# First chunk of a windowed-attention and gated-convolution kernel taken from plain fp32 to three reduced passes, with a ring of 27 blocks for the late queries and keys

## The chip, the cores and the metric

The kernel runs on one core of a Trainium2 chip. The metric is the device time of one execution, in microseconds (us); lower is better. Times of before are given as the median of three executions.

## What is computed

The reference has two halves. The first is causal attention with a window of 128 tokens and a linear distance bias, for 8 batches, 8 heads, 576 tokens and 64 columns per head:

```python
scores = scale * np.matmul(q, k.transpose(0, 1, 3, 2))
rel = pos[:, None] - pos[None, :]
mask = (rel >= 0) & (rel < window)
scores = np.where(mask, scores + bias[None], -1000000000.0)
attn = softmax(scores); attn_out = np.matmul(attn, v)
```

The heads are then laid side by side to x of 4608 tokens by 512, and the second half is a gated network with a depthwise convolution of three taps along the tokens of a batch:

```python
h = np.maximum(x @ w_in, 0.0)                  # 512 -> 1024
conv_out = sum(conv_w[k] * hp[:, k:k + S, :] for k in range(3))
out = h * sigmoid(conv_out) @ w_out            # 1024 -> 512
```

The inputs q and k are scaled so that the scores are large; the weights of the network come as float64 and are decoded on the chip.

## The kernel before

**Tiles and chunks.** Attention goes by 36 tiles `t` of 128 tokens. The network goes by 18 chunks `c` of 256 tokens (two tiles), and within a chunk by four steps, `s = 4c .. 4c+3`, each of two blocks of 128 of the 1024 inner columns. `up(s, ff)` is x times w_in (PSUM tile `p`), `relu`, `middle`, `conv_side` (twice), `tanh` and `gate` make the gated value `z`, `g_hi` and `g_lo` split z into a high and a low half (`gh`, `gl`), and `down(s)` multiplies by w_out into the PSUM tiles `o`.

**Two ways to multiply.** Steps of chunks 1 to 17 multiply in three reduced-precision passes over halves: high weight by high data, high weight by low data, low weight by high data (line 697 in `up`, line 804 in `down`). The halves of x lie in a ring of two chunks, `ring`, filled by `x_hi` and `x_lo`; the halves of the weights are `wi`, `wo` (high, `w_hi`) and `wl` (low, `w_lo`). Chunk 0 (`s < NFP`, with NFP = 4) multiplies in plain fp32, by the whole decoded weight `wg` and by whole data, one matmul in the program per block:

```python
if s < NFP:
    nc.tensor.matmul(
        ps, wgs[b].bitcast(F32)[:, part], x_first[:, cc], start=cc == 0, stop=cc == NCC - 1
    )
    continue
```

A plain fp32 matmul stands as two rows in the profile.

**The weights.** Sixteen blocks of weights and one of taps come by DMA into staging tiles (`wst`, 6 buffers) and are decoded by `w_clamp` (POOL), `w_rebias` (ACT), `w_low` (ACT or DVE), `w_bits` (DVE), `w_hi` (ACT or POOL) and `w_lo` (POOL or DVE).

**Queries and keys.** Tiles 0 to 7 are loaded by `load` and turned by TensorE (`qkT`). From tile 8 on they are loaded in blocks of 32 tokens by 32-row pieces and turned on DVE by `turn` (line 365). A group is 9 blocks (`GB = 9`) in a tile `rp_late` with two buffers: 32 DMAs of 36 KB a group, line 315, emitted by `load_some` where the order has an `LG4`. All DMAs are issued by SP, in order, as are the scratch write of the attention weights (`scr`), the four skewed reads of it (`rr`), the values (`rv`) and the output (`ob`).

**The order.** Nothing is scheduled automatically. Three strings of pieces, `OPENING` (up to about tile 10 and step 9), `PERIOD` (two tiles and one chunk, 14 times) and `TAIL`, are emitted under `tc.manual_schedule`; each engine runs its instructions in that order. A piece is a letter code and numbers: `UH0.1` is `up(0, 1)`, `D5` is `down(5)`, `GH`/`GL` are `g_hi`/`g_lo`, `XH`/`XL` are `x_hi`/`x_lo`, `W` is `w_lo`, `TQ` is `turn`, `WE`/`SE` write and read the scratch, `AV` is attention times values, `S` the scores, `OB` the output. The set `OTHER` names the pieces that `pick` sends to the second of two possible engines.

Of the kernel before, what the change touches and what calls it, by code (L numbers as in the profile page):

```python
# [22 lines left out]
def tile_alibi_window_attention_conv_glu(  # L23
# [71 lines left out]
    mh = apool.tile([P, P], F32, name="mh", tag="qk", bufs=2)  # L95
# [8 lines left out]
    ma = apool.tile([P, P], F32, name="ma", tag="qk", bufs=2)  # L104
# [5 lines left out]
    dist = apool.tile([P, P], F32, name="dist", tag="qk", bufs=2)  # L110
# [16 lines left out]
    for name, cuts in (("start", (96, 64, 32, 0)), ("half", (None, None, 96, 64)), ("after", (32, 0, None, None))):  # L127
        m = apool.tile([P, P], F32, name=f"w_{name}_f", tag="qk", bufs=2)
# [45 lines left out]
    NST = 6  # L174
# [3 lines left out]
    NWL = 18  # L178
# [95 lines left out]
    x_first = apool.tile([P, NCC, XW], F32, name="x_first", tag="xx", bufs=1)  # L274
    nc.vector.memset(x_first[:, :, 0:1], 0.0)
# [13 lines left out]
    TURN = FIRST  # L289

    GB = 9
    groups, turned = {}, [TURN]

    def loads():
        for n in range(TURN * NB // GB, NT * NB // GB):
            lo, hi = max(n * GB, TURN * NB), (n + 1) * GB
            b, s = divmod(lo * BK, S)
            for i, src in enumerate((k, q)):
                for a in range(2):
                    for half in range(D // BK):  # L300
# [22 lines left out]
    def early_raw(t):  # L323
        if t not in raws:
            pair = apool.tile([P, 2, 2, H, D], F32, name=f"rp{t // 2 * 2}", tag="rp", bufs=2)
            for n in range(2):
                raws[t // 2 * 2 + n] = [pair[:, n]]
# [29 lines left out]
    def turn(t):  # L357
        if t < TURN:
            return
        m = 0  # L360
        while m < NB:
            n, at = divmod(t * NB + m, GB)
            assert not waiting or waiting[0][0] > n
            end = min(NB, m + GB - at)
            nc.vector.transpose(
                out=slots_of(t)[:, :, :, m * BK : end * BK].rearrange("p i g (m c) -> p i g m c", c=BK),
                in_=groups[n][:, :, :, at : at + end - m],
            )
            m = end
# [11 lines left out]
    def scores(t, u):  # L381
        if t >= TURN:
            if u == 0:
                for half in range(2):
                    scores_window(t, half)
            return
# [36 lines left out]
    def place(t, u, a):  # L423
# [11 lines left out]
        if t >= TURN:  # L435
# [204 lines left out]
    def x_hi(t):  # L640
# [4 lines left out]
        if t < CT:  # L645
            copy_on(pick(nc.scalar, nc.vector), x_first[:, :, 1 + t * P : 1 + (t + 1) * P], avs.pop(t)[0])
            return
        if t == CT:
            nc.scalar.copy(out=x_first[:, :, 1 + CW : 2 + CW], in_=ps[:, :, 0:1])
        copy_on(pick(nc.scalar, nc.vector), hi, ps)  # L650

    def x_lo(t):
        if t < CT:
            return
# [24 lines left out]
    def up(s, ff):  # L679
        c, f = s // NFP, 2 * (s % NFP) + ff  # L680
        cols = window_x(c)
# [59 lines left out]
    def gate(s, ff=slice(0, 2)):  # L741
        if s not in zgs:
            if s < NFP:
                zgs[s] = fpool.tile([P, 2, CW], F32, name=f"z{s}", tag="gh", bufs=3)
            else:
                zgs[s] = fpool.tile([P, 2, CW], F32, name=f"z{s}", tag="z", bufs=2)
# [5 lines left out]
    def g_hi(s, ff=slice(0, 2)):  # L752
        if s < NFP:
            return
# [6 lines left out]
    def g_lo(s, ff=None):  # L761
        if s < NFP:
            nc.gpsimd.tensor_copy(out=hhs[s][:, :, 0:2], in_=hhs[s][:, :, CW : CW + 2])
            return
# [10 lines left out]
    def down(s):  # L775
# [3 lines left out]
        g = zgs.pop(s) if s < NFP else None  # L779
        gh, gl = gs.pop(s, (None, None))  # L780
# [8 lines left out]
        for ff, m in order:  # L789
# [3 lines left out]
            if s < NFP:  # L793
# [60 lines left out]
    def emit(pieces, t=0, s=0, part=""):  # L854
# [16 lines left out]
        GH6 GH7 GH8 GL5 H14 H15 H16 H2 H5 H9 HH0.0 HH3.1 HH4 HH5 KC7 LW0 LW1 LW10 LW14 LW4 LW8 N2.0 N3.1 N8.0  # L871
        QV2.0 QV3.0 RL1.0 RL3.1 RL5.1 RL6.1 T:GH-1 T:GH0 T:GH1 T:GH2 T:GH3 T:GH4 T:GH5.0 T:GH5.1 T:GL-1 T:GL0
        T:GL4 T:GL5.0 T:HH0 T:HH2 T:HH4 T:HH5.1 T:XL-1 W11 W13 W14 W9 XH0 XH2 XH6
# [88 lines left out]
```

## Time and profile before

| | |
|---|---|
| median of 3 executions | 555.0 us (553.41 to 555.85) |
| the profiled execution | 554.5 us |
| its span in the profile | 552.8 us |
| mean granted TensorE clock, share of full speed | 0.999 |
| PE, DVE, ACT, POOL busy | 546.0, 446.8, 384.4, 342.5 us |
| matmul rows of PE | 6689 |

The span is the time from the first to the last instruction that the profiler saw; some 1.7 us of the execution's time lie outside it. "PE" is TensorE's matmul side and "PEld" its weight loads, which overlap it. Busy time is the union of an engine's instructions. An instruction's own duration includes a tail in which the next one may already run, so that a packed row of instructions takes less than the sum of their durations.

### The profile page before, as it was taken

How to read it: one execution, taken by the hardware profiler on the slowest of the kernel's cores; microseconds unless marked ns; L12 is line 12 of the kernel's file. 1: busy time of each engine (PE TensorE's matmuls, PEld its weight loads, DVE VectorE, ACT ScalarE, POOL GpSimd, SP SyncE). 2: the span in 40 equal slices, each digit the busy share in tenths (PEclk: the TensorE clock that was granted, in tenths of full speed). 3: DMA queues.
4: the chain of work that ended last, by engine and by line, in shares of the span. 5: the costliest groups of instructions: out<-in, count | busy, mean ns of one | idle time of the engine just before them, and what ended most of it. 6: DMA issues, size and time to landing. Idle time of an engine off the chain costs nothing.

```text
span 552.8 us, 17956 instructions
## 1 busy us (share of the span) xinstructions
PE 546.0 (99%) x6689; PEld 479.2 (87%) x6689; DVE 446.8 (81%) x1505; ACT 384.4 (70%) x1149; POOL 342.5 (62%) x450
## 2 busy tenths in 40 slices
PE   9999999999999999999999999999999999999997
PEld 8788886988888888888888888898989898989986
DVE  8899999888789977887596987788879987665763
ACT  5899876775867676868586776767676777664441
POOL 1787977594656575666558493948473948483241
PEclk9999999999999999999999999999999999999999
DMA  9987764546776767767676768676768664540102
GB/s 209 229 242 204 202 104 81 164 156 169 157 205 142 231 156 205 184 205 169 183 201 175 196 178 207 163 219 184 190 176 205 179 162 148 159 155 1 39 0 78
DMA packets 206779, 91.39 MB, mean 165 GB/s; under 512 B 178380, under 2 KB 192996, under 8 KB 206692
## 3 DMA queue, kind: packets, MB, share of 16 engines
q1 hardware_dynamic: 206692, 90.24, 62.5%
q8 instruction: 53, 0.87, 0.7%
q14 instruction: 34, 0.28, 0.2%
HBM read 51.40 MB, written 38.80 MB: 163 GB/s over the span
## 4 chain that ended last, share of the span: by engine, by line
PE 91%; DMA 2%; DVE 2%; SPq 2%; issue 1%; ACT 0%; DVEq 0%
PE o L804 34%; PE p L697 33%; PE av L591 7%; PE sc L413 6%; PE p L692 3%; PE o L794 3%; PE av L631 3%; PE sc L398 2%; SPq L341 1%; DMA wst<-in_moe_w_in_dram 1%; PE pa L507 1%; PE pt L351 1%; DVE zp L732 1%; DMA rp_late<-in_q_dram 1%; SPq L315 0%
## 5 line engine op out<-in xcount | busy, mean ns | idle before, releaser
L697 PE MATMUL p<-ring,wi 128*128 128x256 f32 x1088 | 195.8, 282 | 0.7 <-ACT hh L709 0.7
L732 DVE SCALAR_TENSOR_TENSOR zp<-hh,cw,zp 128x256 f32<-128x256 f32 (+7 forms) x384 | 160.4, 418 | 29.2 <-ACT zp L717 19.6
L697 PEld LDWEIGHTS p<-ring,wi 128*128 128x128 f32 x1088 | 168.4, 188 | 4.9 <-ACT hh L709 1.1
L697 PE MATMUL p<-ring,wl 128*128 128x256 f32 x544 | 152.3, 280 | 0.0
L768 POOL TENSOR_TENSOR gl<-z,gh 128x512 fp32r<-128x512 f32 x63 | 81.5, 1294 | 100.9 <-ACT gh L186 68.4
L481 ACT ACTIVATE e<-e,st 128x128 f32<-128x128 f32 x288 | 111.8, 391 | 4.2 <-DVE st L473 3.1
L804 PE MATMUL o<-wo,gh 128*128 128x512 f32 x270 | 110.0, 407 | 0.0
L501 POOL TENSOR_TENSOR e<-e,st 128x512 f32<-128x512 f32 x69 | 72.2, 1056 | 58.9 <-DVE st L493 54.1
L804 PE MATMUL o<-wo,gl 128*128 128x512 f32 x270 | 105.7, 392 | 0.0
L804 PE MATMUL o<-wl,gh 128*128 128x512 f32 x270 | 105.2, 390 | 0.0
L697 PEld LDWEIGHTS p<-ring,wl 128*128 128x128 f32 x544 | 102.7, 189 | 0.0
L739 ACT ACTIVATE zp<-zp 128x512 f32<-128x512 f32 (+1 forms) x73 | 42.2, 578 | 62.9 <-DVE zp L732 61.5
L717 ACT ACTIVATE zp<-hh,cw 128x256 f32<-128x256 f32 x144 | 68.5, 476 | 20.0 <-DVE z L747 10.0
L473 DVE CUSTOM_DVE_ANT_0 e<-sc,bias 128x128 f32<-128x128 f32 x288 | 66.8, 284 | 1.7 <-PE pa L507 0.2
L747 DVE SCALAR_TENSOR_TENSOR z<-zp,hh 128x512 f32<-128x512 f32 (+1 forms) x73 | 49.0, 671 | 21.1 <-ACT zp L739 20.2
L804 PEld LDWEIGHTS o<-wo,gh 128*128 128x128 f32 x270 | 50.6, 188 | 16.6 <-issue 6.7
L804 PEld LDWEIGHTS o<-wo,gl 128*128 128x128 f32 x270 | 50.5, 187 | 11.5
L804 PEld LDWEIGHTS o<-wl,gh 128*128 128x128 f32 x270 | 50.8, 188 | 9.3
L709 ACT ACTIVATE hh<-p 128x512 f32<-128x512 f32 (+2 forms) x69 | 39.5, 572 | 25.2 <-PE p L697 20.3
L481 ACT ACTIVATION_READ_ACCUMULATOR e<-e,st 128x1 f32 x288 | 54.5, 189 | 0.0
L186 ACT CAST gh<-z 128x512 fp32r<-128x512 f32 x58 | 35.6, 614 | 15.3 <-DVE z L747 15.3
L572 POOL TENSOR_SCALAR_AFFINE_SELECT rr<-rr 128x512 f32<-128x512 f32 x56 | 40.2, 722 | 3.4
(131 smaller groups left out, 882.5 us busy)
## 6 DMA issues: line engine op xcount, KB each, us to landing
scr<-eb SPq DMA_DIRECT2D x28, 1024.0 KB, 5.1
rr<-scr SPq DMA_DIRECT2D x112, 128.0 KB, 3.7
out_dram<-ob SPq DMA_DIRECT2D x17, 512.0 KB, 3.4
rv<-in_v_dram SPq DMA_DIRECT2D x32, 256.0 KB, 3.4
rp_late<-in_k_dram SPq DMA_DIRECT2D x192, 36.0 KB, 2.9
rp_late<-in_q_dram SPq DMA_DIRECT2D x192, 36.0 KB, 2.2
wst<-in_moe_w_in_dram SPq DMA_DIRECT2D x8, 512.0 KB, 7.0
wst<-in_moe_w_out_dram SPq DMA_DIRECT2D x8, 512.0 KB, 4.8
```

The lines of the kernel that those rows point to most:

```text
L473: nc.vector.tensor_tensor_reduce(out=e[:, j, :], in0=of[:, g, :], in1=bias[:, u * HU + j, :], scale=-0.125, scalar=FAR, op0=ALU.add, op1=A ...
L481: nc.scalar.activation(out=e[:, j, :], in_=e[:, j, :], func=AF.Exp, bias=st[:, 0, j : j + 1], scale=-1.0, accum_out=st[:, 1, j : j + 1],)
L501: eng.tensor_tensor(out=e, in0=e, in1=st[:, 2, :].unsqueeze(2).to_broadcast([P, HU, P]), op=ALU.mult)
L572: nc.gpsimd.affine_select(out=r, in_=r, pattern=[[BK, 2], [0, H], [1, BK]], compare_op=ALU.is_ge, fill=0.0, base=q0, channel_multiplier=-1,)
L697: nc.tensor.matmul(ps, a[:, part], ring[:, i, cc, cols], start=cc == 0 and n == 0, stop=cc == NCC - 1 and n == 2)
L709: nc.scalar.activation(out=to, in_=ps, func=AF.Relu, scale=0.5)
L717: nc.scalar.activation(out=zps[s][:, ff, :], in_=hhs[s][:, ff, 1 : 1 + CW], func=AF.Copy, scale=cw[:, 1, f : f + 1])
L732: nc.vector.scalar_tensor_tensor(out=z[:, ff, a:cut], in0=hh[:, ff, a + kk : cut + kk], scalar=cw[:, kk, f : f + 1], in1=z[:, ff, a:cut], ...
L739: nc.scalar.activation(out=zps[s][:, ff], in_=zps[s][:, ff], func=AF.Tanh)
L747: nc.vector.scalar_tensor_tensor(out=zgs[s][:, ff], in0=zps[s][:, ff], scalar=1.0, in1=hhs[s][:, ff, 1 : 1 + CW], op0=ALU.add, op1=ALU.mult,)
L768: eng.tensor_tensor(out=gl, in0=zgs.pop(s), in1=as32(gh), op=ALU.subtract)
L804: nc.tensor.matmul(to, a[:, ff, ms], w[:, part], start=first and n == 0, stop=end and n == 2)
```

## The change

Chunk 0 loses its fp32 way: `up`, `down`, `x_hi`, `x_lo`, `g_hi` and `g_lo` treat it as the other chunks, with the column before the first token set to zero in `ring`. The staging and ring tiles are laid out anew (5 staging buffers and 17 for weights, in place of 6 and 18). Late queries and keys go into one ring of 27 blocks; a load takes up to a batch's 18 blocks. `LG4` becomes `LG2`. `OPENING`, `PERIOD`, `TAIL` and `OTHER` are written anew.

```diff
-    NST = 6
+    NST = 5
-    NWL = 18
+    NWL = 17
...
-    x_first = apool.tile([P, NCC, XW], F32, name="x_first", tag="xx", bufs=1)
-    nc.vector.memset(x_first[:, :, 0:1], 0.0)
+    nc.vector.memset(as32(ring)[:, :, :, 2:3], 0.0)
...
-    GB = 9
-    groups, turned = {}, [TURN]
+    RB = 27
+    raw_ring = cpool.tile([P, 2, H // 2, RB, BK], F32, name="rp_all")
+    turned = [TURN]
 
     def loads():
-        for n in range(TURN * NB // GB, NT * NB // GB):
-            lo, hi = max(n * GB, TURN * NB), (n + 1) * GB
-            b, s = divmod(lo * BK, S)
+        first, per = TURN * NB, S // BK
+        while first < NT * NB:
+            at = (first - per * 2) % RB
+            n = min(per - first % per, RB - at)
+            b, s = divmod(first * BK, S)
...
+            first += n
...
-            if not waiting or waiting[0][0] - 2 >= turned[0] * NB // GB:
+            if not waiting or waiting[0][0] - RB > turned[0] * NB:
                 return
-            n, m, i, p, g, src = waiting.pop(0)
-            if n not in groups:
-                groups[n] = apool.tile([P, 2, H // 2, GB, BK], F32, name=f"rp{n}_late", tag="rp", bufs=2)
-            nc.sync.dma_start(out=groups[n][p : p + BK, i, g, m:], in_=src)
+            _, dst, src = waiting.pop(0)
+            nc.sync.dma_start(out=dst, in_=src)
...
     def x_lo(t):
-        if t < CT:
-            return
         ps, hi, lo = avs.pop(t)
...
     def up(s, ff):
         c, f = s // NFP, 2 * (s % NFP) + ff
-        cols = window_x(c)
+        cols = window_x(c) if c else slice(2, 4 + CW)
...
-            if s < NFP:
-                nc.tensor.matmul(
-                    ps, wgs[b].bitcast(F32)[:, part], x_first[:, cc], start=cc == 0, stop=cc == NCC - 1
-                )
-                continue
...
     def g_hi(s, ff=slice(0, 2)):
-        if s < NFP:
-            return
...
     def g_lo(s, ff=None):
-        if s < NFP:
-            nc.gpsimd.tensor_copy(out=hhs[s][:, :, 0:2], in_=hhs[s][:, :, CW : CW + 2])
-            return
...
-            if s < NFP:
-                nc.tensor.matmul(
-                    oos[c][m], g[:, ff, ms], wgs[b].bitcast(F32), start=f == 0, stop=f == NFC - 1
-                )
-                continue
...
-        T:GL4 T:GL5.0 T:HH0 T:HH2 T:HH4 T:HH5.1 T:XL-1 W11 W13 W14 W9 XH0 XH2 XH6
+        GH0 GH5 GH7 GH8 GL2 GL3 GL7 GL8 H12 H3 H7 HH2.0 HH2.1 HH7 HH8 LW13 LW4 N0.0 N2.1 N6.1 N8.0 P:GH1 P:GH2
...
-    PERIOD = """
-    OB0 HH0 Z0.0 MB2.0.1 MB2.0.0 X2.0.0 UH1.1 UH1.0 HH1 X2.0.1 CA0.0 AV-1 TQ3 CB0.0 XA-1 XS-1 AV0 LG4 GH-1 GL-1 N2.0
+    PERIOD = """
+    UH1.1 MB2.0.0 HH0 MB2.0.1 Z0.1 TQ3 Z0.0 UH1.0 KC3 GH-1 CA0.0 CB0.0 HH1 X2.0.1 AV-1 OB27 CA0.1 X2.0.0 AV0 XA0
```

The pieces of the three orders are the same but for the added `XL0`, `XL1`, `GH0` to `GH3` in `OPENING`; their sequence differs. Two places follow at which the prediction speaks of it.

TensorE, the first `up` of chunk 0. Before, after the transposes of tile 5 (`pt`), the eight instructions of step 0 begin with the first two blocks of weights, `wg`:

```order
L351 MATMUL pt_0_619<-ident_r,rp_444 128x128 x4
L692 MATMUL p_0_663<-x_first,wg_390 128x258
L692 MATMUL p_0_663<-x_first,wg_551 128x258
L692 MATMUL p_0_663<-x_first,wg_556 128x258
L692 MATMUL p_0_663<-x_first,wg_554 128x258
```

and now, after the transposes of tile 6:

```order
L355 MATMUL pt_1_705<-ident_r,rp_674 128x128 x4
L688 MATMUL p_1_717<-ring,wi 128x258 x2
L688 MATMUL p_1_717<-ring,wl_624 128x258
L688 MATMUL p_1_717<-ring,wi 128x258 x2
L688 MATMUL p_1_717<-ring,wl_664 128x258
L688 MATMUL p_1_717<-ring,wi 128x258 x2
L688 MATMUL p_1_717<-ring,wl_672 128x258
```

Four instructions have become twelve (the last two are not shown), and they read the low halves `wl` of four blocks, which had no reader before chunk 1.

SP's queue, the loads for tile 22 and what is issued among them. Before, nine blocks to a load, four loads at a place (`ob` is the output, `eb` the attention weights, `scr` their scratch):

```order
L315 DMA rp_late<-in_k_dram 32x9x32 x4
L544 DMA scr_4141<-eb_4040 256x1x1024
L315 DMA rp_late<-in_k_dram 32x9x32 x4
L558 DMA rr_4227<-scr_3883 32x4x256 x4
L558 DMA rr_4280<-scr_4141 32x4x256 x4
L315 DMA rp_late<-in_k_dram 32x9x32 x4
L341 DMA rv_4297<-in_v_dram 128x8x64
L315 DMA rp_late<-in_k_dram 32x9x32 x4
L315 DMA rp_late<-in_q_dram 32x9x32 x8
L830 DMA out_dram<-ob_4356 128x2x512
```

and now, eighteen blocks to a load:

```order
L547 DMA scr_4189<-eb_4053 256x1x1024
L317 DMA rp_all<-in_k_dram 32x18x32 x8
L345 DMA rv_4340<-in_v_dram 128x8x64
L561 DMA rr_4354<-scr_4189 32x4x256 x4
L317 DMA rp_all<-in_k_dram 32x18x32 x8
L317 DMA rp_all<-in_q_dram 32x18x32 x8
L547 DMA scr_4418<-eb_4352 256x1x1024
L807 DMA out_dram<-ob_4420 128x2x512
L317 DMA rp_all<-in_q_dram 32x18x32 x8
L345 DMA rv_4543<-in_v_dram 128x8x64
```

The 32 loads of this group are each of twice the size and stand in three bunches between two turns. Over the program SP issues 527 DMAs in place of 655: 288 late loads, in nine groups of 4, 18, 9, 9, 18, 18, 9, 9 and 18 blocks, in place of 416 in thirteen groups of 4 and then 9.

## Rows read from the trace of the kernel before

**Rows 1.** The page, part 1: busy time of each engine.

```profile
PE 546.0 (99%) x6689; PEld 479.2 (87%) x6689; DVE 446.8 (81%) x1505; ACT 384.4 (70%) x1149; POOL 342.5 (62%) x450
```

**Rows 2.** Waits of PE: engine, line, waited for: us, times, longest us.

```profile
PE pt L351 <- DVE st L473: 1.1, 1, 1.1
PE p L697 <- ACT hh L709: 0.7, 2, 0.4
```

**Rows 3.** Windows: stretch, busy of PE, PEld, DVE, ACT, POOL, clock, DMA share.

```profile
0.00:20.00 20.00, 17.66 (x158) 16.15 (x158) 16.69 (x102) 13.22 (x45) 6.32 (x15) 1.00 0.92 212
20.00:120.00 100.00, 99.70 (x979) 82.41 (x977) 91.47 (x292) 81.18 (x255) 78.22 (x103) 1.00 0.66 162
349.60:377.90 28.30, 28.30 (x405) 25.17 (x404) 23.79 (x83) 20.45 (x62) 19.71 (x26) 1.00 0.68 206
```

**Rows 4.** Chain of waits in order of time, chunks 0 and 1: start, length, engine, line.

```profile
36.23 3.68 PE p L692 x16
...
66.77 3.63 PE o L794 x8
...
78.37 1.44 PE p L697 x12
...
92.64 3.44 PE o L794 x8
...
103.18 2.75 PE o L804 x12
...
125.12 2.96 PE o L804 x12
```

**Rows 5.** Chain of waits, steady periods, from one tile's `av` to the next.

```profile
206.83 2.84 PE av L591 x128
...
235.10 2.84 PE av L591 x128
...
263.38 1.57 PE av L591 x64
...
271.03 3.96 DMA rp_late<-in_q_dram
...
291.84 2.84 PE av L591 x128
...
321.37 2.84 PE av L591 x128
```

**Rows 6.** Groups of instructions: line, engine, tiles, shape, count | busy us, mean ns.

```profile
L659 DVE TENSOR_TENSOR ring<-av,ring 128x512 fp32r<-128x512 f32 x6 | 4.1, 678 | 0.5 <-ACT ring L186 0.5
L244 DVE TENSOR_TENSOR wl<-wg,wo 128x512 fp32r<-128x512 f32 x4 | 2.7, 684 | 0.0
L221 DVE TENSOR_SCALAR wst<-wst 128x512 uint32<-128x512 uint32 x5 | 3.0, 604 | 1.3 <-DMA wst<-in_moe_w_in_dram 1.3
L188 DVE COPY rl<-pa 128x512 f32<-128x512 f32 x4 | 2.7, 671 | 0.0
L188 POOL CAST gh<-z 128x512 fp32r<-128x512 f32 x9 | 6.3, 701 | 16.6 <-DVE z L747 13.9 <-DVE hh L711 2.7
```

**Rows 7.** Chain of waits, one packed DVE copy of the opening.

```profile
24.11 0.61 DVE rl L188
```

**Rows 8.** Tile `rp_late`: issue min/median/max ns; DVE idle until it, times; landing.

```profile
L315 SPq DMA_DIRECT2D rp_late<-in_k_dram x208: 311/455/2208, 27.7 to 418.6; - x104
...
  DMA rp_late<-in_q_dram: 4.6, 3
...
DMA to landing us min/median/max: 1.8/2.7/7.7
```

**Rows 9.** SP's queue in order of time: start, length, line, DMA, count.

```profile
268.33 3.23 SPq L315 DMA_DIRECT2D rp_late<-in_q_dram  x4
```

**Rows 10.** Lines 768 and 225 alone: duration min/median/max ns.

```profile
L768 DVE TENSOR_TENSOR gl<-z,gh x4: 682/684/1084, 100.6 to 542.4; 128x512 fp32r<-128x512 f32 x4
L225 DVE SCALAR_TENSOR_TENSOR wg<-wg,wst x16: 677/694/1266, 23.2 to 89.8; 128x512 uint32<-128x512 uint32 x16
```

More of the change, by code (lines that the diff above doesn't have):

```diff
@@ L324, in early_raw @@
         if t not in raws:
-            pair = apool.tile([P, 2, 2, H, D], F32, name=f"rp{t // 2 * 2}", tag="rp", bufs=2)
-            for n in range(2):
-                raws[t // 2 * 2 + n] = [pair[:, n]]
+            if t < 6:
+                flat = raw_ring.rearrange("p i g m c -> p (i g m c)")[:, t * 2 * H * D : (t + 1) * 2 * H * D]
+                raws[t] = [flat.rearrange("p (i h d) -> p i h d", i=2, h=H)]
+            else:
+                raws[t] = [wpool.tile([P, 2, H, D], F32, name=f"rp{t}", tag="wst", bufs=NST)]
         return raws[t][0][:, 0], raws[t][0][:, 1]
@@ L359, in turn @@
             return
+        assert not waiting or waiting[0][0] - waiting[0][1].shape[1] >= (t + 1) * NB
         m = 0
         while m < NB:
-            n, at = divmod(t * NB + m, GB)
-            assert not waiting or waiting[0][0] > n
-            end = min(NB, m + GB - at)
+            at = (t * NB + m - 2 * S // BK) % RB
+            n = min(NB - m, RB - at)
             nc.vector.transpose(
-                out=slots_of(t)[:, :, :, m * BK : end * BK].rearrange("p i g (m c) -> p i g m c", c=BK),
-                in_=groups[n][:, :, :, at : at + end - m],
+                out=slots_of(t)[:, :, :, m * BK : (m + n) * BK].rearrange("p i g (m c) -> p i g m c", c=BK),
+                in_=raw_ring[:, :, :, at : at + n],
             )
-            m = end
+            m += n
         turned[0] = t + 1
@@ L381, in scores @@
     def scores(t, u):
[L382 to L385, printed above, removed]
+        if t >= FIRST:
+            for half in range(2) if t >= SOLO else (u,):
+                scores_window(t, half)
             return
@@ L434, in place @@
         ps = sms[t, u][2][a]
-        if t >= TURN:
+        if t >= FIRST:
             place_window(t, ps)
@@ L742, in gate @@
         if s not in zgs:
-            if s < NFP:
-                zgs[s] = fpool.tile([P, 2, CW], F32, name=f"z{s}", tag="gh", bufs=3)
-            else:
-                zgs[s] = fpool.tile([P, 2, CW], F32, name=f"z{s}", tag="z", bufs=2)
+            zgs[s] = fpool.tile([P, 2, CW], F32, name=f"z{s}", tag="z", bufs=2)
         nc.vector.scalar_tensor_tensor(
@@ L918, in tile_alibi_window_attention_conv_glu @@
+    UH3.0 UH3.1 MP3.1.1 GT1 MB3.0.0 MB3.1.1 X3.0.0 MB3.0.1 S4.0 D0 GH1 GL1 D1 CA2.1 CB2.1 CA2.0 LG2 CB2.0 CE1.0
+    MP4.1.0 X3.0.1 MP4.1.1 N3.0 X3.1.0 X3.1.1 N3.1 LG2 LG2 MB4.1.1 LG2 TH2 MB4.1.0 X4.1.1 LV2 GT2 GH2 GL2 HH3 Z3.0
+    TE3.0 SE2 LG2 LG2 UH4.0 CE1.1 XF-1 LG2 LG2 Z3.1 LG2 LG2 LG2 TE3.1 CA3.0 LG2 X4.1.0 CA3.1 CB3.1 CB3.0 MP4.0.0
+    CE2.1 CE2.0 N4.1 UH4.1 WE3 OB0 OB1 MP4.0.1 TH3 GT3
     """
     TAIL = """
-    AV-1 HH0 Z0.0 UH1.1 XA-1 UH1.0 XS-1 D-2 Z0.1 CA0.1 CA0.0 CB0.1 CB0.0 TH0 GT0 XH-1 XL-1 GH-1 XF-1 GL-1 HH1 Z1.1
@@ L926, in tile_alibi_window_attention_conv_glu @@
+    CA1.0 CB1.0 Z1.1 CA1.1 UH4.1 CB1.1 UH2.0 TH1 GH-1 GL-1 UH2.1 GT1 D-2 D-1 HH2 Z2.1 Z2.0 CA2.0 CB2.0 UH3.0 CA2.1
+    CB2.1 GH1 GH0 GL0 TH2 GT2 GH2 UH4.0 D0 GL2 GL1 HH4 HH3 Z3.0 Z3.1 CA3.1 CB3.1 CA3.0 CB3.0 TH3 GT3 GH3 GL3 D1 Z4.1
+    Z4.0 HH5.0 OB1 CA4.1 CB4.1 CA4.0 CB4.0 UH5.1 TH4 HH5.1 GT4 D2 D3 Z5.0 CA5.0 GH4 CB5.0 TH5.0 GT5.0 GL4 D4 Z5.1
+    CA5.1 CB5.1 GH5.0 TH5.1 GT5.1 GL5.0 GH5.1 GL5.1 D5 OB5
     """
@@ L930, in tile_alibi_window_attention_conv_glu @@
         emit(OPENING)
-        for t in range(FIRST, NT, 2):
-            emit(PERIOD, t, 2 * (t - FIRST) + 10, "P:")
-        emit(TAIL, NT, 2 * (NT - FIRST) + 10, "T:")
+        for t in range(SOLO, NT, 2):
+            emit(PERIOD, t, 2 * (t - SOLO) + 10, "P:")
+        emit(TAIL, NT, 2 * (NT - SOLO) + 10, "T:")
 _INS = ["q", "k", "v", "moe_w_in", "moe_conv_w", "moe_w_out"]
```

106 lines of the change are left out of this document (47 added, 59 removed).

## The prediction

> **What bounds the kernel now.** I read four views in this order. The page's first part [rows 1] shows PE busy for 546.0 of 552.8 us; the next engine, DVE, has 446.8. A busy PE need not be a PE at work, so the waits of PE come second [rows 2]: after the first 20 us its longest are 0.7 us on the `hh` of a later chunk and one of 1.1 us at the very start of that stretch. The windows [rows 3] put the lost time in its place: 2.3 us of the first 20 us, 0.3 us of the next 100, none in a steady period, at a granted clock of 1.00 (the 2.4 GHz level) in each. The chain of waits in order of time [rows 4, 5] then runs from one piece of PE's work to the next almost without a break from 25 us to 549 us. So PE's own work sets the time: what is taken off PE comes off the end, as long as the other engines keep ahead of it. The one break in the steady part is around 271 us, where the chain leaves PE for a load of late queries [rows 5]. One period takes 235.10 - 206.83 = 28.27 us; the two at the break take 291.84 - 263.38 = 28.46 and 321.37 - 291.84 = 29.53 us. They lose 1.45 us together.
>
> **Chunk 0 on PE.** Before, 64 rows of plain fp32 `up` (32 matmuls of the program, two rows each): 16 of them take 3.68 us on the chain [rows 4], 0.230 each, so 64 take 14.7 us. Instead there are 96 passes. A pass of 256 columns takes 1.44 / 12 = 0.120 us [rows 4]; with 258 columns, 0.121 us, and 96 take 11.6 us. Saved: 3.1 us. `down` has four steps of 3.63 to 3.44 us [rows 4], mean 3.54, together 14.1 us; a three-pass step takes 2.75 to 2.96 us, mean 2.85, together 11.4 us. Saved: 2.7 us. Both are on the path: **-5.8 us**. Nothing else of PE's work changes: the scores, transposes and idle matmuls keep their number.
>
> **The work this puts on the other engines in the opening.** Chunk 0 now needs two `x_lo`, four `g_hi`, four `g_lo`, and the low halves of its weights at once; `OTHER` also moves pieces. DVE gets, net, three `gl` (0.684 each [rows 10]), two `x_lo` (0.678), four `wl` (0.684) and three copies or products of 512 columns (about 0.67), and gives away two copies of `rl` (0.671) and four `wst` (0.604) [rows 6]: 2.05 + 1.36 + 2.74 + 2.01 - 1.34 - 2.42 = 4.4 us. From 20 to 120 us it is busy 91.5 of 100 us [rows 3]; 95.9 us would have to fit in 94.2, which by these sums it does not. But durations overlap: the packed copy on the chain takes 0.61 us [rows 7] where the mean is 0.671 [rows 6]. At 0.06 us or more an instruction, 292 instructions [rows 3] hold 17 us of tail that a packed DVE does not pay; some 78 of 94 us are really needed. So I take the DVE load as hidden by PE on the whole; if that cover is gone, up to all 5.8 us are. POOL loses work in the opening (four `wl`, three `w_hi`, against one `gl` and one cast more), and ACT, at 81 of 100 us, gains some ten instructions of about the same 0.6 us, for which it has room.
>
> **One new wait, at the first `up`.** It now needs, besides x of tiles 0 to 2, the low halves of four weight blocks and of x. Before it DVE does three `wl` and two `x_lo` more and two `wst` less, 2.05 + 1.36 - 1.21 = 2.2 us, and the transposes, scores and `av` behind which it hides are few. Bounds: nothing, or all 2.2 us, PE standing in order with everything behind it. Early waits of PE on DVE were 1.1 us [rows 2]; I take **+1.0 us**. No other place is charged: a gain at the start (the first 20 us lose 2.3 us, and loads of tiles 4 and 5 need no longer wait for a buffer) is possible up to 1.1 us, and taken as none.
>
> **The late loads.** 128 DMAs less are issued; at 0.455 us each [rows 8] SP has 58 us less to do, 4 us a period. Before, four loads took 3.23 us near the break [rows 9], 0.81 each: the queue ran late there, and DVE waited 4.6 us in three places for loads [rows 8]. I expect the 1.45 us mostly back: **-1.2 us**. Against that stand the groups of 18 blocks. After tile 20 is turned, the 32 loads, a `scr` write, values, four `rr` and an output have about a period, 28.3 us, until tile 22 is turned. Thirty-two issues at 0.455 to 0.81 us are 14.6 to 25.9 us, the others about 3.5, the landing 2.7 [rows 8]: 21 to 32 us. Lateness is bounded by 0 and 4 us in each of two tight groups, and DVE has 28.3 - 23.8 = 4.5 us of room a period [rows 3]: nothing is charged. `GH1` and `GH2` of each period go from ACT to POOL, 28 casts of 0.70 us [rows 6]; POOL has 28.3 - 19.7 = 8.6 us of room a period, and `down` stands some 7 us of PE's work behind `gate`: nothing.
>
> **Sum.** 554.5 (the profiled execution's own time) - 5.8 + 1.0 - 1.2 = **548.5 us**. The median of the executions shown, 555.0, is 0.5 above the profiled one, within their spread; I leave the number there.
>
> **A rule that speaks against it.** Of the four `gl` on DVE one took 1.084 us against a median of 0.684, of sixteen `w_bits` one 1.266 against 0.694 [rows 10]: instructions of two SBUF operands are sometimes held up by 0.4 to 0.57 us. The Trainium skill, "GPSIMD Engine Reference", section 8 (Key points), says that GpSimd shares its SBUF interfaces with VectorE and that they contend when a DVE instruction has two SBUF inputs. That agrees with these rows as far as they go, and this change puts seven more such instructions on DVE in the opening. At the median they cost what is charged above; if each were held up by the larger excess, DVE would get 7 x 0.57 = 4 us more in the opening.
>
> **Rivals.**
> 1. *The opening becomes DVE's.* For it: 95.9 us of DVE rows in 94.2 us. Against it: the tails, and no wait of PE on DVE worth naming after 25 us. If DVE sets the pace of the opening, the 5.8 us are not seen there and only the break is won: 554.5 - 1.2, with the first `up` inside it, 553.3 us; half of it gives 551.
> 2. *The long loads come late, and the kernel is slower.* Place: the turns of tiles 22 and 31. If an issue of 72 KB cost twice the 0.81 us, 32 of them with the rest would take 52 + 6 = 58 us in a period of 28.3: 30 us late, less 4.5 of room, 25 us for each: 548.5 + 50 = 598. The size of a load would have to govern the time of its issue; lateness begins at (28.3 - 6.2) / 32 = 0.69 us an issue, a loss of more than the gain at about 0.93 us. With 1.0 us: 38 us, 10 late, 5.4 lost twice, 559 us. For it: 0.81 us was seen [rows 9]. Against it: the median is 0.455 [rows 8] and half as many issues carry a block.
> 3. *Held-up DVE.* The contention of the paragraph above in the opening, with DVE already close: 548.5 + 4 = 552.5 us.
> 4. *Three passes are not cheaper,* because loading their weights paces them. Excluded but for a remnant: 12 passes in 1.44 us are on the chain already. It would give 554.
>
> **How the numbers follow.** My forecast, 546 to 550.5: 0.66. Rival 1: 0.19, half of it on each side of 552. Rival 2: 0.08. Rival 3: 0.05. Rival 4: 0.02. The range leaves out rival 2 and the worse end of rival 1: 554.5 - 5.8 - 1.45 - 1.1 = 546.1, rounded down to 546.0, to 553.0. About 0.5% is what a measurement of this kernel can tell from no change, so faster means under 552.2: the forecast, half of rival 1 and a part of rival 3, 0.77. Within it: the rest of them and rival 4, 0.15. Slower, over 557.8: rival 2, 0.08.
>
> **What would show it.** In the profile after: no plain fp32 rows, 1728 passes of `up` at about 0.12 us; PE busy some 6 us less, its share still 99%; chunk 0's four `down` at 2.75 to 2.96 us; a wait of PE of a microsecond or so just before the first `up`; the period still 28.27 us; DVE's waits for late loads under 5 us in all. Wrong would be: PE waits of several us on `z`, `gl` or `ring` between 40 and 120 us (rival 1 or 3), or a DVE wait of over 5 us at line 369 near tiles 22 and 31, followed by PE (rival 2).

## The result, and the profile after

The changed kernel takes **560.7 us** (median of 4 executions, 559.38 to 562.34) against 555.1 us before (553.41 to 555.85): a ratio of 1.0107, 95% interval 1.0071 to 1.0143. It is 1% slower; the forecast was 548.5 us, the range 546 to 553. Between forecast and result stand 12.2 us.

Part 1 of the page of after, beside [rows 1]:

```profile
PE 546.1 (97%) x6737; PEld 483.1 (86%) x6737; DVE 450.7 (80%) x1505; ACT 378.8 (68%) x1131; POOL 354.1 (63%) x471
```

PE has 48 matmul rows more, none of them plain fp32, and is no less busy; its share fell from 99% to 97% since the span grew by 7.8 us. Where, the windows of after tell (length, then PE, PEld, DVE, ACT and POOL busy, the granted clock, DMA share, GB/s), beside [rows 3]:

```profile
0.00:20.00 20.00, 17.69 (x155) 15.85 (x156) 17.83 (x107) 13.51 (x52) 4.68 (x14) 1.00 0.91 231
20.00:40.00 20.00, 15.71 (x194) 13.59 (x195) 16.77 (x58) 16.23 (x48) 16.11 (x20) 1.00 0.81 189
40.00:60.00 20.00, 18.89 (x176) 17.08 (x176) 17.71 (x49) 16.96 (x56) 13.16 (x17) 1.00 0.75 179
60.00:120.00 60.00, 59.41 (x632) 51.58 (x632) 55.24 (x171) 49.11 (x143) 43.65 (x59) 1.00 0.75 147
```

PE lacks 4.3 us from 20 to 40 us, 1.1 in the next 20 and 0.6 in the 60 after; before, 0.3 in all of it. The waits of PE in after from 20 to 128 us (us in total, times, longest), beside [rows 2], spread that over three engines:

```profile
PE av L634 <- DVE st L476: 1.7, 1, 1.7
PE pa L510 <- POOL e L504: 1.5, 1, 1.5
PE sc L401 <- ACT rl L186: 1.0, 1, 1.0
PE pa L510 <- DVE qkT_all L188: 0.9, 1, 0.9
```

The chain of after in order of time (start, duration, what) shows two of these waits from behind, beside [rows 4] and [rows 7]. PE's transposes at 22.68 wait for POOL, which had clamped a weight (`wst`) and masked an attention tile before it came to scale `e`. The scores at 31.39 wait for ACT, which had first two `wst`, a `wi` and a `wg` to make:

```profile
20.36 0.66 POOL wst L204
21.02 0.59 POOL rl L524
21.61 1.02 POOL e L504
22.68 0.66 PE pa L510 x4
...
28.63 1.17 ACT wst L219 x2
...
30.30 0.56 ACT wg L214
30.86 0.48 ACT rl L186
31.39 1.17 PE sc L401 x14
```

The first `up` starts at 43.3 us instead of 36.1. Tile 8's `av`, where the opening ends, starts at 127.91 us on the chain of after; before it started at 123.6. So the opening, from which 5.8 us of PE's work were to be taken, got 4.3 us longer in this execution, which is the slowest of the four (562.34 us). In seven variants below that leave the order of the opening as it is, that `av` starts at 124.4 to 127.0, 0.8 to 3.4 us later than before. The rest of the miss lies later, in the chain of after:

```profile
182.90 2.84 PE av L594 x128
199.86 5.76 PE o L781 x24
211.29 2.84 PE av L594 x128
...
296.03 2.84 PE av L594 x128
...
309.25 6.52 DMA scr<-eb
...
318.30 4.05 DMA rr<-scr
...
328.09 1.57 PE av L594 x64
...
355.22 2.84 PE av L594 x128
```

A steady period takes 211.29 - 182.90 = 28.39 us, 0.12 more than before [rows 5], and two `down` steps take 5.76 where the chain of before has 5.69 (at 281.90 and 311.43 us). The two periods from 296.03 take 59.19 us, 2.4 more than two periods: a scratch write that lands only after 6.52 us, the reads `rr` of 4.05, and PE's `av`, which waits for them. SP's queue in order of time (start, length, line, DMA, count) shows why they come late. DVE was done with the blocks `eb` of that write at 301.7 us; the write was issued at 309.25, behind eight late loads, and its reads at 317.69, behind eight more and two loads of values:

```profile
299.94 6.66 SPq L317 DMA_DIRECT2D rp_all<-in_q_dram  x8
...
309.25 0.52 SPq L547 DMA_DIRECT2D scr<-eb  x1
309.87 6.27 SPq L317 DMA_DIRECT2D rp_all<-in_k_dram  x8
...
317.69 1.99 SPq L561 DMA_DIRECT2D rr<-scr  x4
```

PE's wait for `rr` and DVE's for late loads, in the whole execution of after, beside [rows 8]:

```profile
PE av L594 <- POOL rr L575: 2.2, 1, 2.2
DVE qkT_all L369 <- DMA rp_all<-in_q_dram: 6.8, 2, 4.3
```

The two turns that waited for loads stand at 278.0 and 413.3 us; behind the first no wait of PE follows, behind the second PE stands 0.8 us, for nothing that the profile shows. So there are three places to explain: the opening, the period, the late loads. Landmarks below are the starts of tile 8's `av` (before 123.6, after 127.9) and of the `av` of tiles 11 and 12 (before 178.5, after 182.9). Medians of the kernel before in the jobs below are 554.4 to 554.8 us.

### The profile page after: what moved, and what is told of

Its sections match the earlier page's. It is cut to its first block, busy times and chain, and to the rows that moved or that the text cites. A ratio compares the mean times of both kernels' runs of the same rounds, so it can differ in the third digit from the quotient of the medians.

```text
span 560.6 us, 17953 instructions
## 1 busy us (share of the span) xinstructions
PE 546.1 (97%) x6737; PEld 483.1 (86%) x6737; DVE 450.7 (80%) x1505; ACT 378.8 (68%) x1131; POOL 354.1 (63%) x471
## 4 chain that ended last, share of the span: by engine, by line
PE 87%; DVE 4%; POOL 2%; DMA 2%; ACT 1%; issue 1%; SPq 0%; DVEq 0%; POOLq 0%
PE o L781 35%; PE p L688 33%; PE av L594 7%; PE sc L416 6%; PE av L634 3%; PE sc L401 2%; DMA scr<-eb 1%; DVE e L476 1%; PE idle L72 1%; DVE sc L445 1%; PE pt L355 1%; POOL wl L244 1%; DMA rr<-scr 1%; PE pa L510 1%; DVE zp L723 1%
## 5 line engine op out<-in xcount | busy, mean ns | idle before, releaser
L688 PE MATMUL p<-ring,wi 128*128 128x256 f32 (+1 forms) x1152 | 207.7, 282 | 0.6 <-DVE ring L661 0.3
L688 PEld LDWEIGHTS p<-ring,wi 128*128 128x128 f32 x1152 | 178.7, 188 | 4.6 <-DVE ring L655 0.5
L688 PE MATMUL p<-ring,wl 128*128 128x256 f32 (+1 forms) x576 | 161.6, 280 | 0.0
L781 PE MATMUL o<-wo,gh 128*128 128x512 f32 x286 | 117.0, 409 | 0.0
L781 PE MATMUL o<-wl,gh 128*128 128x512 f32 x286 | 113.0, 395 | 1.0 <-issue 0.8
L781 PE MATMUL o<-wo,gl 128*128 128x512 f32 x286 | 112.8, 394 | 0.0
L688 PEld LDWEIGHTS p<-ring,wl 128*128 128x128 f32 x576 | 108.8, 189 | 0.0
L708 ACT ACTIVATE zp<-hh,cw 128x256 f32<-128x256 f32 x144 | 68.9, 479 | 51.8 <-DVE zp L723 38.5
L700 ACT ACTIVATE hh<-p 128x512 f32<-128x512 f32 (+1 forms) x70 | 40.0, 572 | 27.9 <-PE p L688 27.1
L537 DVE STREAM_TRANSPOSE eb<-e 128x512 f32<-128x512 f32 x56 | 38.7, 702 | 7.5 <-DMA rp_all<-in_q_dram 4.2
L369 DVE STREAM_TRANSPOSE qkT_all<-rp_all 128x1024 f32<-128x1024 f32 (+3 forms) x31 | 35.1, 1136 | 10.9 <-DMA rp_all<-in_q_dram 6.8
```

The costliest lines, as they stand in the source:

```text
L688: nc.tensor.matmul(ps, a[:, part], ring[:, i, cc, cols], start=cc == 0 and n == 0, stop=cc == NCC - 1 and n == 2)
L700: nc.scalar.activation(out=to, in_=ps, func=AF.Relu, scale=0.5)
L708: nc.scalar.activation(out=zps[s][:, ff, :], in_=hhs[s][:, ff, 1 : 1 + CW], func=AF.Copy, scale=cw[:, 1, f : f + 1])
L781: nc.tensor.matmul(to, a[:, ff, ms], w[:, part], start=first and n == 0, stop=end and n == 2)
```

## Experiments

### The opening: one part of the change in the old order

Two theories. **A**: the new order of the opening is at fault. **B**: the early halves are. A third, **C**, is rival 1 made wider: any added split work costs its own time because the other engines stand as close to the limit as PE.

**The old order with all of chunk 0 in three passes.** `XL0`, `XL1`, `GH0` to `GH3` added, splits moved up to their first reader:

```diff
-UH1.0 UH1.1
+H2 H3 W0 W2 W3 UH1.0 UH1.1
...
-D0
+H9 W9 H10 W10 D0
...
-D1
+H11 W11 H12 W12 D1
```

> The kernel before, with its ring, loads, period and tail, and chunk 0 alone put into three passes: the low halves of tiles 0 and 1 and the high and low halves of gate steps 0 to 3 are added, and the splits of the weight blocks are moved ahead only as far as their first reader asks. Theory A (the wholly new order of the opening is at fault): the trace of after lost about 10 us in the opening by its order, so the old order keeps most of the 5.8 us of passes: 549 to 552 us. Theory B (the early halves themselves are at fault: the first `up` can't start until four weight blocks and two tiles are split, about 7 us later, and until then the PE has no bulk work to fill its waits with): the old order loses as much: 556 to 561 us, and the first `up` starts near 43 us.

Measured 584.4 us, ratio 1.0537 (1.0510 to 1.0563). (In this order the second half of step 2's `up` stands behind `XH4`, and so reads tile 4's columns of the ring in place of tile 0's.) Theory A is out by 32 us, and the first `up` starts at 39.6, not 43. PE waits 7.3 us for `wo` from ACT and 4.2 for `wl` from DVE: the moved splits themselves. More is lost behind such a wait: after 6.0 us in which PE stood for `wo`, the granted clock was 0.50 (the 1.2 GHz level) from 104.4 to 109.5 us, and a pass of `down` took 0.43 us from start to start where it takes 0.23 at 1.00. The mean granted clock of this execution is 0.979.

**Only `down` in three passes.**

```diff
-D0
+H9 W9 H10 W10 D0
...
-D1
+H11 W11 H12 W12 D1
```

> The kernel before with only the `down` of chunk 0 in three passes; its `up` stays in fp32 and starts as early as before. Theory B (early halves for `up` cost the time): `down` needs its halves 30 us later, when the splits can be hidden, so 2.7 us of passes go and nothing comes: 552 to 553 us, first `up` still at 36 us. Theory A: the same 552 to 553. A third, C (any added split work in the opening costs its own time because DVE, ACT and POOL bound it together): 555 to 558 us.

Measured 566.6 us, ratio 1.0213 (1.0190 to 1.0236): worse than C said. The first `up` starts as early as before, but PE waits for `wo`, 5.2 us in two waits. Both kernels move splits without finding them a good place, so neither prices the halves alone; the next ones do.

**PE's saving alone.** The fp32 matmuls become three passes over the same operands, with nothing else changed:

```diff
-                    ps, wgs[b].bitcast(F32)[:, part], x_first[:, cc], start=cc == 0, stop=cc == NCC - 1
+                for n in range(3):
+                        ps, wgs[b].bitcast(BF16)[:, 1::2][:, part], x_first[:, cc].bitcast(BF16)[:, 1::2],
```

> The kernel before, in which chunk 0's `up` and `down` are three bfloat16 passes over the upper half-words of the same operands (`wg`, `x_first`, `z`), at the places and behind the waits of the fp32 matmuls: PE's saving alone, with no half to make and no order changed. Chunk 0's values are wrong by this (three times a product of the truncated operands). If PE sets the pace of the opening, as the prediction has it, 5.8 us go: 549 us. If DVE, ACT and POOL are right behind PE there (rival 1), less goes: 551 to 554 us, and PE waits for them between 40 and 120 us.

Measured **554.6 us, ratio 1.0002** (0.9984 to 1.0020), 12 executions. A saving of 5.8 us on an engine that was busy for 99% of the span is worth nothing, to within 1 us. The saving was there: from 20 us to tile 8's `av`, PE's rows, each taken at the median distance to the next start of its kind, come to 98.3 us in before and 92.7 here, and the time beyond that grew from 5.1 to 9.6 us (worked out from the starts in both traces). The busy time hides this and fell by 3.7 us only, to 542.3: a row's duration covers short gaps (an fp32 row of `up` lasts 0.381 us, and the next starts after 0.230). Tile 8's `av` starts at 122.4, 1.2 us early; that of tiles 11 and 12 at 178.3, 0.2 early. The reason stood in the trace of before, in a view that the prediction does not use: what the *others* wait for in the opening. The waits of DVE and, below, two of ACT's in before, 40 to 122 us:

```profile
DVE zp L732 <- ACT zp L717: 1.4, 3, 0.5
DVE z L747 <- ACT zp L739: 1.3, 3, 0.6
DVE eb L534 <- POOL e L501: 1.2, 1, 1.2
DVE hh L711 <- PE p L692: 0.7, 1, 0.7
...
ACT rl L186 <- PE pa L507: 2.2, 1, 2.2
...
ACT hh L709 <- PE p L692: 1.3, 2, 1.1
```

In 82 us DVE waits for PE once, for 0.7 us, but for 0.2 us more at a short transpose. ACT does wait for PE, 4.8 us in all; in this experiment 1.1 us of that are left, and ACT's waits for DVE grow from 11.8 to 15.4 us. What ACT no longer waits for PE, it waits for DVE. With PE's passes cheaper the chain simply runs elsewhere. From the chain of this experiment:

```profile
37.83 0.77 ACT e L482 x4
...
50.48 0.61 ACT zp L742
51.11 0.69 DVE z L750
...
91.83 1.15 DVE qkT_all L366
```

**Is it DVE alone?** The same kernel without chunk 0's outer taps:

```diff
 def conv_side(s, ff, kk):
+    if s < NFP:
+        return
```

> The fifth experiment's kernel (PE's saving alone) in which chunk 0 leaves out its two outer taps: 16 products fewer on DVE, some 7 us of its rows, in the opening; nothing less on PE. There the saving brought tile 8's `av` forward by only 1.2 us (122.4 against 123.6), and the chain of waits runs through DVE and ACT. If the opening is DVE's once PE's passes are cheaper, tile 8's `av` starts 3 to 4.6 us sooner than that, at 118 to 119.5 us. If something else holds it (the loads of weights, ACT alone), it stays at 122 us.

Measured 553.2 us, ratio 0.9976 (0.9955 to 0.9996); tile 8's `av` at 122.1. Seven us of DVE's busy time gone brought 0.3 us there. DVE alone is not what holds the opening; its chain now passes from engine to engine:

```profile
56.98 2.77 PE p L694 x24
...
66.47 5.36 DMA wst<-in_moe_w_out_dram
...
72.90 1.59 ACT e L482 x8
...
86.18 1.87 SPq L316
...
91.55 1.15 DVE qkT_all L366
```

PE, the weights' DMA, ACT, SP's queue and DVE each hold a stretch. How far each of them stands behind PE was not measured.

**The added halves, unread.** The old order with PE's saving, plus chunk 0's two `x_lo`, four `g_hi` and four `gl`, which nothing reads:

```diff
-XH0
+XH0 XL0
...
-GT0
+GT0 GH0
```

> The fifth experiment's kernel (old order, PE's saving alone) with the halves of chunk 0's data made as well, though nothing reads them: two `x_lo` on DVE, four `g_hi` (three on ACT, one on POOL), four `gl` (two on POOL, two on DVE), each right behind the piece that gives its input. Chunk 0's values are wrong as in the fifth. The fifth reached tile 8's `av` at 122.4 us, before at 123.6, the changed kernel and its variants at 125.2 to 127.8. If every engine is right behind PE in the opening, these ten instructions of 0.55 to 1.3 us come on top: tile 8's `av` at 124 to 126 us, the time 556 to 558 us. If the other engines have room for them: 122.4 and 554.5 us, and the opening of the changed kernel is slow by its order alone.

Measured **560.0 us, ratio 1.0099** (1.0082 to 1.0117), 5.4 us above the saving alone. Tile 8's `av` starts at 128.6. PE now waits, 20 to 140 us:

```profile
PE pt L352 <- DVE st L474: 3.1, 2, 1.9
PE av L632 <- POOL rl L522: 1.7, 2, 1.0
PE sc L399 <- ACT qkT_all L187: 0.7, 1, 0.7
```

Ten instructions of 0.61 to 1.73 us, 9.0 us of rows on three engines of which the busiest, DVE, had been busy for 91.4 of the 100 us from 20 to 120 in the fifth experiment, cost 5.4 us. **Of them only the two `x_lo`:**

```diff
-GT0 GH0
+GT0
```

> The thirteenth experiment's kernel with only the two unread `x_lo` of tiles 0 and 1 (DVE, about 0.68 us each, ahead of the first `up`) and none of chunk 0's `g_hi` and `gl`. Chunk 0's values are wrong as in the fifth. The thirteenth reached the first `up` at 39.7 us against 36.3 in the fifth, and tile 8's `av` at 128.6 against 122.4. If DVE's chain before the first `up` is what sets it, the two instructions alone bring the first `up` to 38 to 40 us and tile 8's `av` to 124 to 125.5 us, 556 to 557 us. If the halves of `z` cost all of it: 36.3, 122.4 and 554.6 us.

Measured 557.2 us, ratio 1.0046 (1.0024 to 1.0067): 2.6 us above the saving alone for two instructions of 0.69 us; first `up` at 38.5, tile 8's `av` at 124.4. From its chain, the piece before the first `up`: the second `x_lo` (`ring`) delays the biases (`sc`, `e`) by which PE's next transposes are released.

```profile
33.24 0.60 ACT x_first L187
33.86 0.69 DVE ring L656
34.55 0.34 DVE sc L443
...
37.75 0.20 DVE e L474
...
38.02 0.67 PE pt L352 x4
```

So B and C hold in one: the halves of x cost 2.6 us for 1.4 us of rows, those of z 2.8 us for 7.6 us of rows, each difference known to some 1.5 us. One part of B is not borne out:

**The low halves of the first weights made later,** in the changed kernel (chunk 0's third pass takes the high half again):

```diff
-((blocks[b][1], 0), (blocks[b][1], 1), (wls[b], 0))
+((blocks[b][1], 0), (blocks[b][1], 1), (wls[b] if c else blocks[b][1], 0))
...
-W0 X3.1.0
+X3.1.0
...
-UH5.1
+W0 W1 W2 W3 UH5.1
```

> The changed kernel in which chunk 0's `up` takes the high half of the weight in its third pass too (as many passes, of the same size), so that the low halves of the first four weight blocks (`W0` to `W3`, three on DVE, one on POOL) need not be made before the first `up`, and stand behind tile 4's work, ahead of chunk 1's `up`. Chunk 0's `up` lacks the product with the weights' low halves. Theory B (the early halves hold the first 43 us up): the first `up` starts about 2 us sooner and the time falls by 1.5 to 3 us: 558 to 559 us. Theory A (it is the order of attention's pieces on the other engines that holds PE up, not these four): 560 to 561 us.

Measured 563.4 us, ratio 1.0162 (1.0142 to 1.0181). The first `up` started at 40.9, but seven other kernels with the changed opening, its splits unmoved, started it at 40.1 to 41.9; nothing was won there. The time is 2.7 us above the changed kernel; that the four splits cost this at their new place is likely, but not shown.

### The period: 32 bytes

**A pad behind `xx`,** whose buffer the change made 32 bytes shorter by dropping `x_first`:

```diff
-xx.append(apool.tile([P, 2, H // 2, P], F32, name="xx", tag="xx", bufs=1))
+xx.append(apool.tile([P, 2 * H // 2 * P + 8], F32, name="xx", tag="xx", bufs=1))
```

> The changed kernel with 32 bytes a partition added behind the buffer `xx`, so that the buffers allocated after it (`gh`, `gl`, `wl`, the staging) start where 32 bytes more put them, as in the kernel before, whose `x_first` was 32 bytes longer than `xx`. In the traces one pass of `down` on `wo`, `gl` takes 233.6 ns from start to start in after, in the first experiment (which lost `x_first` as well) and in the third and fourth, and 229.5 in before and in the second. If the place of those buffers sets this, the passes go back to 229.5 ns, the period to 28.27 us, and some 14 x 0.12 = 1.6 us go: 559 us. If the passes are slower for another reason: 560.7 us and 233.6 ns.

Measured **558.0 us, ratio 1.0062** (1.0044 to 1.0080), 2.7 us less than the changed kernel. Its chain:

```profile
197.89 5.69 PE o L782 x24
209.25 2.84 PE av L594 x128
...
237.52 2.84 PE av L594 x128
```

Two steps of `down` take 5.69 again, the period 28.27; the passes on `wo`, `gl` went from 233.4 back to 229.1 ns, as the mean from start to start. **The other way round, before with 32 bytes more:**

```diff
-x_first = apool.tile([P, NCC, XW], F32, name="x_first", tag="xx", bufs=1)
+x_first = apool.tile([P, NCC * XW + 8], F32, name="x_first", tag="xx", bufs=1)
```

> The kernel before with 32 bytes a partition added behind `x_first`, so that the buffers allocated after it move by 32 bytes, the other way round from the sixth experiment. If the place of those buffers sets the speed of `down`, the passes on `wo`, `gl` go from 229.5 to 233.6 ns, the period from 28.27 to 28.39 us, and the time rises by 1.6 to 2.7 us: 556.5 to 557.5 us. If the slower passes have another cause in the changed kernel: 229.5 ns and 554.8 us.

Measured 557.3 us, ratio 1.0051 (1.0034 to 1.0068), 234.5 ns in place of 229.2. The place of the buffers alone does it.

### The late loads

**The old period and tail in the changed kernel:**

```diff
-UH1.1 MB2.0.0 HH0 MB2.0.1 Z0.1 TQ3
...
+OB0 HH0 Z0.0 MB2.0.1 MB2.0.0 X2.0.0
...
```

> The changed kernel with the period and the tail of before (their order and engine choices), all else as changed. The trace of after has a steady period of 28.39 us against 28.27 and a tail about 0.5 us longer. If these two lists cost what the landmarks say (12 periods x 0.12 us, 0.5 us of tail), the time is 558 to 559 us. If the late loads' stalls come from the new period's order, another 1 us goes: 557 us. If all of the loss is in the opening: 560.5 us.

Measured 567.1 us, ratio 1.0232 (1.0207 to 1.0257): 6 us worse than the changed kernel, against every expectation. The period stayed at 28.4 us (the buffers, not the order), and DVE waited 15.6 us for late loads. The new period belongs to the new ring.

**Hardly any late loads in the changed kernel:**

```diff
-waiting = list(loads())
+waiting = list(loads())[: 3 * 32]
```

> The changed kernel with only the first three late loads (31 blocks); later turns read what is left in the ring. From tile 16 on queries and keys are not those of the tile. All waits for late loads are gone, and their DMA traffic with them. The landmarks of after give 2.4 us of break near 300 us and 0.6 near 420: if the late loads cost that, 557 to 558 us; if they are hidden: 560.5 us.

Measured 556.4 us, ratio 1.0039 (1.0025 to 1.0053): late loads cost the changed kernel 4.3 us, by the waits above more through `rr` than through the turns. **The same cut in before:**

```diff
-waiting = list(loads())
+waiting = [x for x in loads() if x[0] < 6]
```

> The kernel before with only the first three groups of late queries and keys loaded; later turns read the last two groups again, so from about tile 14 on queries and keys are not the tile's. The same cut took 4.3 us off the changed kernel (eighth experiment). If the ring of longer loads made the late loads dearer, less goes here: the break of 1.45 us, 553 us. If late loads cost before as much: 550.5 us.

Measured 553.8 us, ratio 0.9989 (0.9976 to 1.0002): 1.0 us. So 3.3 us of the 4.3 are new. **And in the kernel with PE's saving alone,** by the same edit:

> The fifth experiment's kernel (PE's saving alone) with only the first three groups of late queries and keys loaded; later turns read the last two groups again, so from about tile 14 on queries and keys are not the tile's. The fifth gained 1.2 us up to tile 8 and stood level with before again at tile 18, after two periods of 29.3 and 29.4 us. If the late loads took the gain back, no period is over 28.4 us here and the time is 555 - 1.2 - 1.45 - the rest of the breaks, 551.5 to 552.5 us. If another thing did: 554.5 us.

Measured 553.2 us, ratio 0.9976 (0.9962 to 0.9991). One period of 30.1 us was left, in which PE stood 1.5 us for nothing that the profile shows, so late loads are not all that takes such a gain back.

**Size of a load and quota of issues.** Four kernels by these edits, one or both, with LG3 or LG4:

```diff
-n = min(per - first % per, RB - at)
+n = min(per - first % per, RB - at, 9)
...
-LG2
+LG4
```

> The changed kernel with late loads of at most 9 blocks in place of 18 (more loads, as many bytes, a quota of two for each place in the order as before). If the long loads come late because they are long, the turns that waited 6.8 us in all wait less and the time falls by 1 to 2.5 us, to 558.5 to 559.5 us. If the loads are late for another reason (issue quota, place in the queue), nothing falls, or more comes: 560.5 to 563 us.

> The sixth experiment's kernel (the changed one with 32 bytes more behind `xx`) with late loads of at most 9 blocks and four issues at each place of the order in place of two. In a ring of 27 blocks a load of 18 may start only when the ring holds 9 unturned blocks, one period ahead of need; a load of 9 may start with 18 blocks left. If the late loads come late by that (and the fourth experiment was slow only for its quota of issues), the breaks near tiles 17 and 26 go: 558.0 - 3 = 555 us. If they come late because SP's queue or the DMA engines are full: 558 us or more.

> The sixth experiment's kernel with loads of up to 18 blocks as in the changed kernel, but four issues at each place of the period in place of two: a load that may start is issued within half a period in place of a whole one. If the slow quota makes them late: 555.5 to 556.5 us. If the permission to start comes too late whatever the quota: 558 us.

> The sixth experiment's kernel (32 bytes more behind `xx`) with late loads of at most 9 blocks and three issues at each place of the period (48 a period, as before the change), the opening's places as in the changed kernel. Nines with two a place fell behind (fourth experiment), and four a place held up the reads of the scratch behind them in the queue (eleventh, twelfth). If there is a quota between that serves both, no DVE wait for `rp_all` over 2 us and no PE wait for `rr` over 2 us in all: 554.5 to 556 us. If bursts of loads and the reads of the scratch collide at any quota that keeps up: 560 us or more, with PE waiting for `rr`.

| kernel | largest load, blocks | issues a place | DVE waits for `rp_all`, us | PE waits for `rr`, us | us (ratio) |
|---|---|---|---|---|---|
| padded (sixth) | 18 | 2 | 7.9 | 1.0 | 558.0 (1.0062) |
| fourth, no pad | 9 | 2 | 8.7 | 8.5 | 572.4 (1.0306) |
| fifteenth, padded | 9 | 3 in the period | 4.2 | 21.9 | 587.2 (1.0589) |
| twelfth, padded | 18 | 4 in the period | 0.6 | 23.3 | 586.2 (1.0553) |
| eleventh, padded | 9 | 4 everywhere | 0 | 16.5 | 594.0 (1.0723) |

The gain hoped for came in none of the four; they miss it by 13 to 39 us. In the eleventh and the fifteenth the other branch came true, that the queue is full or that loads and reads of the scratch collide. Where the loads are issued faster, DVE's waits for them go, and PE's appear at the other end. PE in the twelfth:

```profile
PE av L594 <- POOL rr L575: 23.3, 6, 7.6
```

The loads and the reads `rr` of the scratch go through one queue, SP's. What makes the loads early makes `rr` late, and `rr` stands nearer to PE. (In the eleventh the opening's loads crowd the weights too: tile 8's `av` at 142.3 us.) The waits are not the whole price: the mean granted clock is 0.994 in the fourth and 0.977 to 0.982 in the other three, where the padded kernel has 1.00. The changed setting, 18 blocks by twos, is the best of those tried.

### Both single costs taken away together

The sixth's edit and the eighth's in one kernel:

> The changed kernel with both single costs taken away: 32 bytes more behind `xx` (sixth experiment, -2.7 us) and only the first three late loads (eighth, -4.3 us; from tile 16 on queries and keys are not the tile's). If the two are independent the time is 560.7 - 2.7 - 4.3 = 553.7 us, level with the kernel before under the same cut of loads (553.8, fourteenth): what is left, three passes, halves and new order, is then worth nothing either way. If the breaks only take turns (one covers the other), 555 to 556 us.

Measured **553.8 us, ratio 0.9987** (0.9972 to 1.0003), 553.7 expected: the two are independent. With the sixth and the eighth this gives each cost a second time, and by the ratios' intervals more surely than against the four executions of the changed kernel, which leave each open by some 2 us: the pad without late loads is worth 2.9 us (known to 1.2), the late loads with the pad 4.2 (known to 1.3). The kernel before without late loads is at 553.8 too. What is left of the change, three passes, their halves and the new order, is worth nothing either way, to within some 1 us.

## Why the prediction was wrong

The 11.6 us between the forecast change (-6.0) and the measured one (+5.6) come from three terms, 12.0 us by the experiments: the opening, 0 for -4.8 (4.8); the late loads, +3.3 for -1.2 (4.5); the place of the buffers, +2.7, in no term. The 0 for the opening is what the eighteenth kernel leaves; there tile 8's `av` starts at 124.35, 0.8 us later than before. The 4.3 us that the profile of after shows there are of its slowest execution and are not all in the median.

- *"So PE's own work sets the time: what is taken off PE comes off the end, as long as the other engines keep ahead of it."* **This step failed**, and with it the sum. It was read from [rows 1 to 4], which show that PE rarely waits. They do not show that the others have time to spare, and busy time with its tails covers short waits. The condition in its second half was the question, and the fifth experiment answers it: 5.6 us less of PE's rows up to tile 8's `av`, which starts 1.2 us earlier, and 0 in the time.
- *Chunk 0 on PE, -5.8.* The sizes were right. Before, `down` of chunk 0 took 3.54 us a step; in after its four steps start at 81.8, 87.0, 99.6 and 102.4 us and take 2.8, 2.9, 2.9 and 3.3 (a wait of 0.4 in the last), and the fp32 rows are gone. What it takes from PE does not come off the end.
- *"So I take the DVE load as hidden by PE on the whole."* Failed. The sum of the rows, 95.9 us in 94.2, was right to warn, and the tails by which I made 78 of it were the wrong correction: on DVE, ACT and POOL in order, each waiting for the others, ten instructions cost 5.4 us. The bound was written there ("if that cover is gone, up to all 5.8 us are") and not taken.
- *One new wait at the first `up`, +1.0.* Mis-sized and misplaced. No wait stands at the first `up` to speak of; 5.1 us of waits stand before it, on attention's pieces that queue behind weights' splits on POOL, ACT and DVE.
- *The late loads, -1.2.* Wrong sign. Issues did get fewer, but the median issue (0.496 us) was never the matter: a load of 18 may start only when 9 unturned blocks are left, and at the break two bunches of eight, at 0.83 and 0.78 us an issue, stood before a scratch write and its reads.
- *"The period still 28.27."* 28.39, by 32 bytes. *`GH1` and `GH2` on POOL at nothing*: right, no wait of PE names them.
- *Rivals.* The first was right in kind (no gain seen in the opening) and had 0.19. It took the saving for worth nothing at worst, 553.3 us; with the two other terms taken away the eighteenth kernel is at 553.8. The second named the place, turns of tiles 22 and 31: the break in the chain lies between tiles 20 and 24, the turn near 413 us waits 4.3 us. Its mechanism was right in part: the issues did not take twice 0.81 us, but those of the two bunches before the break are over the 0.69 us at which it let lateness begin, and what they hold up is `rr`, not the turn. The third brought nothing new. [rows 10] show of `w_bits` only the longest; the timeline of before has seven of sixteen over 0.85 us, 3.0 us together above 0.69. In after four `w_bits` (0.80 to 0.95), three `wl` on DVE (0.89, 1.13, 1.47) and a `gl` (0.78) make 2.4 us. Those over 0.80 us had POOL instructions running beside them for 0.4 us or more, and those with none beside them took 0.68 to 0.69. The rule of the Trainium skill, "GPSIMD Engine Reference", section 8 (Key points), that the two engines contend when a DVE instruction has two SBUF inputs agrees with these rows. The fourth was rightly given little.

Theory A is not borne out either. The old order with the halves added is at 560.0, with the better place of buffers and the loads of before; the changed opening with the pad and few loads is at 553.8. By these the new order wins back some 5 us of what the halves cost (an estimate: 560.0 - 1.0 - 553.8). What stays open is which of the waits before 43 us a still better order would remove; no kernel here beats the one before with the whole of the work.

## What to carry to other kernels

A bound engine's share and its lack of waits don't price a saving: ask whether the other engines wait for it, and what they would wait for next. If they wait for each other, replace the operation by a cheaper one at the same place, whatever values it gives, and see what the saving alone is worth before building what it needs. In a kernel whose order is set by hand, a few added instructions can cost the kernel microseconds (two rows of 0.69 us cost 2.6 here), and a quota of loads belongs to the size of a load and to what stands behind it in the queue.

## What the runs showed of the hardware

Thirty-two bytes in the place of the buffers change the speed of matmuls: passes of 512 columns on `wo`, `gl` took 229.1 to 229.2 ns from start to start at one place of `gh`, `gl`, `wl` and the buffers behind them, 233.4 to 234.5 at the other, with the same instructions, and the time of the kernel moved by 2.7 us one way and 3.0 the other. Which passes slow down with them differs: those on `wl`, `gh` in the changed kernel (232.6 against 227.4 with the pad), those on `wo`, `gh` in before with 32 bytes more (233.1 against 230.7). The passes of `down` themselves explain 14 x 0.12 = 1.6 us of the time; the rest, and which of the buffers it is, were not tried. Identical openings differed between kernels by up to 3.2 us at the first `up` (40.1 to 43.3).
